# Block-sparse attention and a three-way feed-forward on one core: early PSUM banks, first weight landings, register loads and planner times changed

## The chip, the cores and the metric

One core of a Trainium2 chip runs the whole program. Its engines are TensorE (PE, with its weight loads counted apart as PEld), VectorE (DVE), ScalarE (ACT), GpSimd (POOL) and the queue of SyncE (SP), which issues most transfers. The metric is the device time of one execution in microseconds, as the median of several runs.

## The reference

Attention over 4 batches of 8 heads with 768 positions of 64 values, in blocks of 32 positions. A block of queries sees its own block and its two neighbours, the first and the last block, and three sampled blocks; the first and the last block of queries see everything. The attention's rows (3072 x 512) then go through a feed-forward with three weight matrices, of whose products the elementwise maximum is taken, and an output matrix.

```python
mask = np.abs(blk_i - blk_j) <= window
mask = mask | (blk_i == 0) | (blk_j == 0) | (blk_i == n_blocks - 1) | (blk_j == n_blocks - 1)
...
scores = np.where(mask, scores, -1000000000.0)
...
return np.matmul(attn, v).astype(np.float32)
...
h = np.maximum(np.maximum(x @ w1, x @ w2), x @ w3)
return (h @ w_out).astype(np.float32)
```

## The kernel before, in words

Every operand of a matmul is held as two float16 parts, a high one and a low one (the rest), after a scaling by a power of two; a product is three passes (high-high, high-low, low-high, `PASSES`). So each fp32 input is first brought into such parts: K, Q and V, and the weights.

**Units.** A batch has 12 units of 64 query rows. Eleven are sparse: unit m takes blocks 1+2m and 2+2m. One, "G", takes the first and the last block against all keys. Their order is G, 10, 8, 9, then 0 to 3, then 4 to 7. A sparse unit gathers its key blocks on chip (`gather`, line 746: per unit six copies of sampled blocks at line 757, one for each of two query blocks and three samples, and two window copies at lines 763 and 765, into tile `kg`) and its value rows from a copy of V in DRAM (`vscr`) by indirect DMAs of the GpSimd queue (line 769, into `vg`). Two items of four heads each follow: scores on PE into a pair of PSUM banks (line 844), row maxima (DVE, line 823), the bias (ACT, line 825), exponentials (ACT, line 853), the high part (ACT, line 801), the low part (POOL or DVE, line 802 or its alternative), a transposing DMA (SP, line 806) into `pts`, and the product with the values (PE, line 868). The global unit does the same with all keys (`global_items`, lines 889 to 923); the first one is turned on PE in place of the DMA (line 794). `finish_unit` (line 933) divides, turns the 64 rows on PE into a PSUM bank (line 950), and writes both parts into `xg`. Every fourth unit completes 256 rows, and a feed-forward follows (`feed_forward`, line 961): 18 groups of 12 matmuls (line 977), and 6 groups for the output (line 1004). There are 12 of them.

**The start.** Constants; the sampled block numbers are loaded into tile `samp`, and from there into engine registers (`registers`, line 396; the load is line 393), which the copies of line 757 use as offsets. Each engine needs registers of its own. Batch 0's K, Q and V land in `stage` and `qn`; their scales come from sums of squares on PE (`gram`, line 422, matmuls at line 430; `total`, line 412, line 418) and a few tiny DVE operations (lines 405 to 410, 607, 706, 707). K and Q are turned on PE (line 602 in the first batch) and evicted by ACT (high part: lines 630 and 719) and DVE (low part: 633 and 722). V's parts are made by ACT (line 648) and DVE (line 652) and stored to `vscr` (line 656). `edges` (line 729) copies the first and last key block into both `kg` buffers (DVE, line 735) and the same of V into both `vg` (SP, line 741).

**Weights.** `prep_weights` takes eight groups of three 512 KB pieces: six groups of w1, w2 and w3, two of w_out. A piece lands by DMA (lines 472 and 475), is decoded (POOL or ACT, lines 479 and 482; DVE, line 486), summed (lines 430 and 418), and split into high (ACT, line 508) and low parts (DVE, line 520, or POOL, lines 518 and 519). `stage_of` says where piece t lands: pieces 0 and 1 in `xg` buffers 1 and 2, then in turn in the six `stage` tiles (also those of K and V) and one `xg`.

**PSUM.** Two score tiles `s_ps0` and `s_ps1` of two banks each, `av_ps`, two banks `f_ps` of the feed-forward, and `tp_ps`. In the planner the score tiles' banks are 0 to 3 and `tp_ps` is 4. A score item takes a pair, (0, 1) or (2, 3). A turn or sum takes a single: bank 4, and while its priority is below `early` = 4, also bank 3 or 2, the two halves of `s_ps1`.

**The order of the work.** Nothing is ordered by hand. Every operation is given to `Plan.add` (line 57) with its engine, an estimated duration `us`, the keys that it reads and writes, a priority `pri` (lower is earlier), for transfers a time `land` from issue to landing and a share `move` of DMA time, and with `alts` other engines that could do it. `Plan.order` (line 81) plays the list through: it gives each engine, whenever it is free, the ready operation of lowest priority; among alternatives it takes the one that ends first. What results is the fixed program order on each engine; on the chip each instruction still waits for its semaphores. `Plan.gaps` finds where PE stands idle in the plan, and `idle` puts dummy matmuls there (line 1079).

Of the kernel before, what the change touches and what calls it, by code (L numbers as in the profile page):

```python
# [32 lines left out]
TP, HOLD, WPRI, WSL = 0.45, 1.0, 1.5, 0.65  # L33
# [10 lines left out]
class Plan:  # L44
# [6 lines left out]
    SEM, DEPTH, START, COLD = 0.15, 2, 2.0, 3.0  # L51
    PACKET, FETCH, QUEUE = 256, 2.2, 0.8

    def __init__(self, early):
        self.ops, self.wrote, self.readers, self.early = [], {}, {}, early

    def add(self, eng, us, emit, r=(), w=(), pri=0.0, land=None, mode=None, move=0.0, take=None, pair=False, drop=None, free=(), port=0, fresh=None, alts=(), n=24, half=False):
# [20 lines left out]
        self.ops.append(Op(eng=eng, us=us, emit=emit, deps=deps, pri=pri, land=land, mode=mode, move=move, take=take, pair=pair, drop=drop, port=port, fresh=fresh, seen=seen, n=n, half=half,  # L78
                           alts=[(eng, us, emit, port), *alts] if alts else ()))

    def order(self, hold, switch):
# [6 lines left out]
        dma, lock, banks = 0.0, 0.0, [0.0] * 5  # L88
# [41 lines left out]
        while len(out) < n:  # L130
# [92 lines left out]
def tile_block_sparse_attention_maxout_ffn(ctx, tc, q, k, v, sampled, w1, w2, w3, w_out, out):  # L223
# [69 lines left out]
    FAR = 1e6  # L293
# [153 lines left out]
    w_first = [(xg[i].rearrange("p g t x -> p (g t x)").bitcast(F32), XK(i)) for i in range(1, 3)]  # L447
    w_first += [(vgf[i][:, 1024 * x : 1024 * x + 1024], VGK(i)) for x in range(2) for i in (1, 0)][:0]
# [53 lines left out]
    def split_w(g, parts, sc, keys, pri):  # L502
        m3, hi, lo, mk = parts
        for k in range(3):
# [11 lines left out]
            else:  # L516
                def low(sl=sl, s=s):
# [4 lines left out]
                    r=keys + [("w", g, k, 0)], w=mkk + [("w", g, k, 1)], pri=pri, port=1, alts=[("POOL", 3.2, low, 0)] if 1 else ())  # L522
# [42 lines left out]
    def load_v(x, b, pri, after):  # L565
        sts = []
        for a in range(3):
# [5 lines left out]
            ), r=after, w=SK(i), pri=pri, land=2.2, move=2.05)  # L573
# [68 lines left out]
    def prep_v(b, pri, after=()):  # L642
        sm = vsm[b % 3]
        sts = load_v(v, b, pri, after)
        kv_scale(sts, sm, "v", b, pri)
        for a in range(3):
# [4 lines left out]
            for e in range(2):  # L651
# [3 lines left out]
                    r=SK(sts[a]) + [("v", "s", b), ("vh", a)], w=[("vl", a, e)], pri=pri, port=1)  # L655
# [382 lines left out]
    F = 0  # L1038
# [77 lines left out]
```

## Time and profile before

| | |
|---|---|
| median of 3 runs | 665.83 us (665.64 to 666.9) |
| the profiled execution, its own time | 669.87 us |
| its span in the trace | 668.1 us |
| mean granted TensorE clock | 0.971 |
| PE busy | 607.5 us, 11033 matmuls (233 of them dummies, 33.5 us) |
| DVE, ACT, POOL busy | 401.9, 415.7, 323.0 us |
| moved by DMA | 105.09 MB |

Times in views are microseconds from the span's start. "L977" is line 977 of the kernel. A view of waits names for each instruction the event that released it; "issue" stands where the engine waited for nothing that the profile shows. A granted clock of 1.00 is full speed.

### The profile page before, as it was taken

What the parts mean: (1) busy time and instruction counts of PE and PEld (TensorE: products, weight loads), DVE (VectorE), ACT (ScalarE), POOL (GpSimd) and SP (SyncE); (2) the same over time, 40 slices, a digit from 0 to 9 for tenths busy, and PEclk for the clock granted to TensorE, in tenths of its full rate; (3) what the DMA queues carried; (4) which work ended last, traced back from release to release, by engine and by line L of the source; (5) the groups of instructions that cost most, each with busy time, mean ns of one, the idle gap of its engine ahead of it and who ended that gap; (6) DMA issues with size and microseconds to landing.
All of it is one profiled execution on the core that took longest, in us unless ns stands there. A gap on an engine that the chain in (4) does not pass through costs nothing.

```text
span 668.1 us, 26145 instructions
## 1 busy us (share of the span) xinstructions
PE 607.5 (91%) x11033; PEld 459.8 (69%) x11033; DVE 401.9 (60%) x963; ACT 415.7 (62%) x898; POOL 323.0 (48%) x414
## 2 busy tenths in 40 slices
PE   6697877989999899999999998999998899988997
PEld 5575556866776676866867756868866768657684
DVE  2386889997775564665766555656865547435221
ACT  0365767898678565685778655775776566635211
POOL 3114755845536473455366644554365565625110
PEclk9897779999999899999999998999999999999999
DMA  7679999999769999997579897863589874784100
GB/s 194 190 235 245 210 226 164 198 196 210 128 99 216 169 161 193 178 164 157 118 179 197 154 191 163 187 154 93 143 186 165 149 167 91 128 124 89 37 14 31
DMA packets 194567, 105.09 MB, mean 157 GB/s; under 512 B 154785, under 2 KB 181522, under 8 KB 194450
## 3 DMA queue, kind: packets, MB, share of 16 engines
q1 hardware_dynamic: 186002, 74.13, 61.0%
q0 software_dynamic: 8448, 29.29, 18.3%
q8 instruction: 86, 1.41, 0.9%
q14 instruction: 31, 0.25, 0.2%
HBM read 62.91 MB, written 12.70 MB: 113 GB/s over the span
## 4 chain that ended last, share of the span: by engine, by line
PE 68%; DMA 9%; issue 7%; DVE 6%; ACT 5%; ACTq 2%; POOL 1%; another core or an unknown queue 1%; SPq 0%; DVEq 0%; POOLq 0%
PE f_ps L977 37%; PE f_ps L1004 11%; PE av_ps L868 6%; DMA pts<-phl 6%; PE s_ps L844 5%; PE tp_ps L599 3%; DMA vg<-vscr,rows_of 2%; ACTq L393 2%; DMA vscr<-vhl 1%; ACT pr L853 1%; PE tp_ps L950 1%; PE s_ps L889 1%; ACT phl L801 1%; PE s_ps L602 1%; PE f_ps L1079 1%
## 5 line engine op out<-in xcount | busy, mean ns | idle before, releaser
L977 PE MATMUL f_ps<-xg,w_hl 128*128 128x256 f16 x2592 | 304.4, 274 | 7.4 <-issue 5.4
L977 PEld LDWEIGHTS <-w_hl 128*128 128x128 f16 x2592 | 249.2, 98 | 48.2 <-issue 17.1
L802 POOL TENSOR_TENSOR phl<-pr,phl 128x512 f16<-128x512 f32 (+1 forms) x112 | 128.8, 1154 | 112.7 <-ACT phl L801 52.4
L990 POOL TENSOR_TENSOR ht<-hf,ht 128x256 f16<-128x256 f32 x72 | 51.8, 719 | 124.8 <-ACT ht L989 123.9
L986 DVE SCALAR_TENSOR_TENSOR hf<-f_ps,hf 128x256 f32<-128x256 f32 x144 | 60.8, 422 | 79.3 <-PE f_ps L977 72.4
L769 POOL DMA_INDIRECT vg<-vscr,rows_of x88 | 84.2, 956 | 48.6 <-PE av_ps L868 27.8
L1004 PE MATMUL f_ps<-wo_hl,ht 128*128 128x512 f16 x432 | 99.4, 379 | 1.3 <-DVE hf L986 1.3
L853 ACT ACTIVATE pr<-s_ps,nm,qsm 128x256 f32<-128x256 f32 x176 | 92.7, 561 | 6.8 <-ACT nm L825 0.4
L823 DVE TENSOR_REDUCE nm<-s_ps 128x2 f32<-128x512 f32 x88 | 59.6, 686 | 32.7 <-PE s_ps L844 27.5
L1004 PEld LDWEIGHTS <-ht 128*128 128x128 f16 x432 | 40.9, 98 | 46.2 <-issue 3.2
L801 ACT CAST phl<-pr 128x512 f16<-128x512 f32 (+1 forms) x112 | 66.7, 596 | 5.4 <-DMA pts<-phl 3.2
L868 PE MATMUL av_ps<-vg,pts 128*32 128x65 f16 (+1 forms) x4224 | 51.9, 197 | 12.5 <-issue 8.2
L868 PEld LDWEIGHTS <-pts 128*32 128x32 f16 x4224 | 41.6, 96 | 30.4 <-issue 24.6
L989 ACT CAST ht<-hf 128x256 f16<-128x256 f32 x72 | 28.9, 401 | 53.6 <-DVE hf L986 53.5
L825 ACT ACTIVATE nm<-nm,ln_top,qsm 128x2 f32<-128x2 f32 x88 | 34.0, 386 | 43.4 <-DVE nm L823 43.4
L844 PE MATMUL s_ps<-kg,qt 64*32 64x256 f16 x2112 | 49.7, 286 | 7.0 <-issue 4.3
L982 ACT ACTIVATE hf<-f_ps 128x256 f32<-128x256 f32 x72 | 27.5, 382 | 33.2 <-PE f_ps L977 30.6
L773 DVE COPY vg<-vg 32x2080 f16<-32x2080 f16 x44 | 38.2, 868 | 11.2 <-DMA vg<-vscr,rows_of 10.1
L757 POOL COPY kg<-kt 128x256 f16 x88 | 38.6, 460 | 12.9 <-DVE kt L633 12.0
L757 ACT COPY kg<-kt 128x256 f16 x104 | 38.0, 402 | 3.2 <-issue 1.5
L844 PEld LDWEIGHTS <-qt 64*32 64x32 f16 x2112 | 25.2, 93 | 20.8 <-issue 14.9
L1079 PE MATMUL f_ps<-ident 128*128 128x256 f16 x233 | 33.5, 299 | 0.0
(164 smaller groups left out, 690.2 us busy)
## 6 DMA issues: line engine op xcount, KB each, us to landing
stage<-in_moe_w_dram SPq DMA_DIRECT2D x14, 511.0 KB
vscr<-vhl SPq DMA_DIRECT2D x12, 520.0 KB
stage<-in_v_dram SPq DMA_DIRECT2D x12, 512.0 KB
out_dram<-ob SPq DMA_DIRECT2D x20, 256.0 KB
stage<-in_k_dram SPq DMA_DIRECT2D x18, 256.0 KB
qn<-in_q_dram SPq DMA_DIRECT2D x17, 256.0 KB
stage<-in_moe_w_out_dram SPq DMA_DIRECT2D x5, 511.8 KB
vg<-vscr SPq DMA_DIRECT2D x16, 130.0 KB
```

The lines of the kernel that those rows point to most:

```text
L757: (A.copy if by == 2 else eng.tensor_copy)(out=dst, in_=src)
L769: plan.add("POOL", 1.02, lambda c=c: L.indirect_dma_start(out=vgj[: (6 - 2 * c) * HB, c].rearrange("p e h x -> p (e h x)"), out_offset=Non ...
L801: plan.add("ACT", 0.05 + 0.565 * n / 512, lambda: A.copy(out=hl[:, :n], in_=prt[:, :n]), r=PRK(it), w=[hk], pri=pri, alts=[("DVE", 0.6 * n ...
L802: plan.add("POOL", 1.2 * n / 512, lambda: L.tensor_tensor(out=hl[:, n : 2 * n], in0=prt[:, :n], in1=hl[:, :n], op=ALU.subtract), r=PRK(it) ...
L823: plan.add("DVE", 0.7, lambda: V.tensor_reduce(out=n[:, 0:2], in_=both()[:, :, :256], axis=AX.X, op=ALU.max), w=[ks, (ks, 0), (ks, 1)], pr ...
L844: T.matmul(out=s_ps[r * BS : (r + 1) * BS, hd * 512 : hd * 512 + 256], lhsT=q_t[hp, tq, 2 * i + u, q0 + c * BS : q0 + (c + 1) * BS], rhs=k ...
L853: plan.add("ACT", 0.56, lambda hd=hd: A.activation(out=prt[:, hd * 256 : hd * 256 + 256], in_=s_of(job)[:, hd * 512 : hd * 512 + 256], fun ...
L868: T.matmul(out=av_ps[r * BS : (r + 1) * BS, 2 * i + hd, :w], lhsT=pv[:, tp, hd, e, r * BS : (r + 1) * BS], rhs=vgj[:, c, e, h, (D + 2) * t ...
L977: T.matmul(out=pf, lhsT=w_hl[f][:, j, g, wp], rhs=x[:, g, xp, :], start=g == 0 and n == 0, stop=g == G - 1 and n == 2)
L986: plan.add("DVE", 0.42, lambda h=h, pf=pf: V.scalar_tensor_tensor(out=h, in0=pf, scalar=2.0 ** -14, in1=h, op0=ALU.mult, op1=ALU.max), r=[ ...
L990: plan.add("POOL", 0.7, lambda h=h, hi=hi, lo=lo: L.tensor_tensor(out=lo, in0=h, in1=hi, op=ALU.subtract), r=[hk, ("ht", f)], w=[("htl", f ...
L1004: T.matmul(out=f2_ps, lhsT=hts[:, f, hp, t * P : (t + 1) * P], rhs=wo_hl[f // 3][:, f % 3, wp], start=f == 0 and n == 0, stop=f == NF - 1 ...
```

## The change

Nothing of what is computed changes. The edits:

- Early singles: `early` goes from 4 to 3, and the banks offered become 4 (`tp_ps`), 5 (`f_ps1`, for operations numbered below `plan.first`), 2 and 0 (the first halves of `s_ps1` and `s_ps0`). `plan.first` is set to 1 after `prep_v(0)`. Operations that free a bank before that are readers of a key "first", on which the first matmuls into `f_ps1` depend.
- Weight pieces 2 and 3 land in `wo_hl[1]` and `wo_hl[0]`, tiles that later hold the output weights.
- Registers: sample 0 goes to DVE (was ACT for the first units), sample 1 stays with POOL, sample 2 with ACT; each loads 8 at first, and POOL and ACT six more in twos. The copies of sample 0 for units 1 to 8 go from ACT to DVE.
- Weights' low parts lose the alternative POOL; batch 0's V low parts get one, in two POOL operations.
- Planner times: transposing DMAs are planned to land 1.5 us later and gathers 2.0 us later (`slack`), the bias operation takes 0.38 in place of 0.22, the modelled depth of SP's queue is 1.5 in place of 2.
- Priorities: weights from 1.5 to 1, unit ends from 5 to 7 ahead, edges from 0.3 to 1 behind, K of the next batch two units earlier, V's loads of batches 2 and 3 released two units later and with the same resulting priority.

```diff
-TP, HOLD, WPRI, WSL = 0.45, 1.0, 1.5, 0.65
+TP, HOLD, WPRI, WSL = 0.45, 1.0, 1, 0.65
...
-    SEM, DEPTH, START, COLD = 0.15, 2, 2.0, 3.0
+    SEM, DEPTH, START, COLD = 0.15, 1.5, 2.0, 3.0
...
             deps.add(drop["op"])
+            if not self.first:
+                self.readers.setdefault("first", []).append(i)
...
-            return [(banks[j], -j, 1) for j in ((4, 3, 2) if ops[i].pri < self.early else (4,))]
+            return [(banks[j], -j, 1) for j in (4, 5, 2, 0) if (ops[i].pri < self.early if j < 4 else j == 4 or i < self.first)]
...
-                done = max(dma, done) + op.land
+                done = max(dma, done) + op.land + op.slack
...
-    plan = Plan(4)
+    plan = Plan(3)
...
-        return tp_one if j == 4 else s_pss[1][:, 512 * (j - 2) : 512 * (j - 1)]
+        return tp_one if j == 4 else f_ps[1] if j == 5 else s_pss[j // 2][:, :512]
...
+    w_late = [wo_hl[1], wo_hl[0], *w_hl[:0:-1]]
+    w_first += [(x.rearrange("p j g t x -> p (j g t x)" if len(x.shape) == 5 else "p f t x -> p (f t x)").bitcast(F32)[:, :1024],
+                 [("w", g, k, t) for k in range(2) for t in range(2)])
+                for g, x in zip((NF + 1, NF, *range(NF - 1, 0, -1)), w_late)][:2]
...
-                    r=keys + [("w", g, k, 0)], w=mkk + [("w", g, k, 1)], pri=pri, port=1, alts=[("POOL", 3.2, low, 0)] if 1 else ())
+                    r=keys + [("w", g, k, 0)], w=mkk + [("w", g, k, 1)], pri=pri, port=1, alts=[("POOL", 2.85, low, 0)] if 0 else ())
...
+        def low_v(x, hi, lo):
+            L.tensor_scalar(out=x, in0=x, scalar1=sm[:, 8:9], scalar2=None, op0=ALU.mult)
+            L.tensor_tensor(out=lo, in0=x, in1=hi, op=ALU.subtract)
...
-                    r=SK(sts[a]) + [("v", "s", b), ("vh", a)], w=[("vl", a, e)], pri=pri, port=1)
+                    r=SK(sts[a]) + [("v", "s", b), ("vh", a)], w=[("vl", a, e)], pri=pri, port=1, alts=[("POOL", 2.85, lambda src=src, a=a, e=e: low_v(src[:, e], vhl[:, a, e, :, :D], vhl[:, a, e, :, D + 2 :]), 0)] if 1 and not b else ())
...
-                by = (2,1,2)[t] if pri < 8 else t
+                by = (0,1,2)[t] if pri < 8 else t
...
-            ), r=VSCR(b) + ["rows_of"] + pace, w=[("vg", j % 2, c)], pri=pri, land=2.5, move=1.6 - 0.5 * c)
+            ), r=VSCR(b) + ["rows_of"] + pace, w=[("vg", j % 2, c)], pri=pri, land=2.5, move=1.6 - 0.5 * c, slack=2.0)
...
-            r=[hk, lk], w=[tk, ("ptl", it % NPT)], pri=pri - 2, land=2.0, move=1.75 * n / 512)
+            r=[hk, lk], w=[tk, ("ptl", it % NPT)], pri=pri - 2, land=2.0, move=1.75 * n / 512, slack=1.5)
...
-        plan.add("ACT", 0.22, lambda: A.activation(
+        plan.add("ACT", 0.38, lambda: A.activation(
...
-        pri -= 5
+        pri -= 7
...
-                         w=[("f1", fb)] + [("pace", F, x) for x in range(4) if (f, j) == ((0, 0), (1, 1), (3, 0), (4, 1))[x]], pri=pri, mode="f", fresh=fb)
+                         w=[("f1", fb)] + [("pace", F, x) for x in range(4) if (f, j) == ((0, 0), (1, 1), (3, 0), (4, 1))[x]],
+                         free=["first"] if F == f == 0 and j == 1 else (), pri=pri, mode="f", fresh=fb)
...
-        by = (2,1,2)[t] if 8 > 0 else t
-        registers(t, by, many if by else many[:8], -9 + t / 10)
+        by = (0,1,2)[t] if 8 > 0 else t
+        first = 8 if by else 8
+        registers(t, by, many[:first], -9 + t / 10)
+        for x in range(first, len(many) if by else first, 2):
+            registers(t, by, many[x : x + 2], 0.5)
...
     prep_v(0, PV)
+    plan.first = 1
...
-            edges(b, U + 0.3)
+            edges(b, U + 1)
...
-        if x == max(gx, 4 if U < 12 else 3) and b + 1 < B:
-            prep_v(b + 1, U + 7, [("unit", U)])
+        if x == max(gx, 4 if U < 12 else 5) and b + 1 < B:
+            prep_v(b + 1, U + 5, [("unit", U)])
...
-            prep_k(b + 1, U + 2, [("unit", U)])
-            turn_k(b + 1, U + 2 + 1)
+            prep_k(b + 1, U + 0, [("unit", U)])
+            turn_k(b + 1, U + 0 + 1)
```

More of the change, by code (lines that the diff above doesn't have):

```diff
@@ L44, with add @@
 class Plan:
-    SEM, DEPTH, START, COLD = 0.15, 2, 2.0, 3.0
+    SEM, DEPTH, START, COLD = 0.15, 1.5, 2.0, 3.0
     PACKET, FETCH, QUEUE = 256, 2.2, 0.8
     def __init__(self, early):
-        self.ops, self.wrote, self.readers, self.early = [], {}, {}, early
-    def add(self, eng, us, emit, r=(), w=(), pri=0.0, land=None, mode=None, move=0.0, take=None, pair=False, drop=None, free=(), port=0, fresh=None, alts=(), n=24, half=False):
+        self.ops, self.wrote, self.readers, self.early, self.first = [], {}, {}, early, 0
+    def add(self, eng, us, emit, r=(), w=(), pri=0.0, land=None, mode=None, move=0.0, take=None, pair=False, drop=None, free=(), port=0, fresh=None, alts=(), n=24, half=False, slack=0.0):
         i = len(self.ops)
@@ L77, in add @@
             take.update(op=i, left=0, end=0.0)
-        self.ops.append(Op(eng=eng, us=us, emit=emit, deps=deps, pri=pri, land=land, mode=mode, move=move, take=take, pair=pair, drop=drop, port=port, fresh=fresh, seen=seen, n=n, half=half,
+        self.ops.append(Op(eng=eng, us=us, emit=emit, deps=deps, pri=pri, land=land, mode=mode, move=move, take=take, pair=pair, drop=drop, port=port, fresh=fresh, seen=seen, n=n, half=half, slack=slack,
                            alts=[(eng, us, emit, port), *alts] if alts else ()))
@@ L87, in order @@
         ready, cands, free, last = [0.0] * n, {}, {}, "f"
-        dma, lock, banks = 0.0, 0.0, [0.0] * 5
+        dma, lock, banks = 0.0, 0.0, [0.0] * 6
         pos, since, back, kept = 0, -9.0, 0.0, None
@@ L284, in tile_block_sparse_attention_maxout_ffn @@
     tp_one = ps.tile([P, 512], F32, name="tp_ps")
-    plan = Plan(4)
+    FAR = 1e6
+    plan = Plan(3)
     def bank(job):
         j = job["banks"][0]
-        return tp_one if j == 4 else s_pss[1][:, 512 * (j - 2) : 512 * (j - 1)]
+        return tp_one if j == 4 else f_ps[1] if j == 5 else s_pss[j // 2][:, :512]
     V, A, T, Y, L = nc.vector, nc.scalar, nc.tensor, nc.sync, nc.gpsimd
-    FAR = 1e6
     SK = lambda i: [("stage", i), ("stage2", i)]
@@ L572, in load_v @@
                 in_=x[b, :, a * 256 : (a + 1) * 256, :].rearrange("h (p e) d -> p h (e d)", e=2),
-            ), r=after, w=SK(i), pri=pri, land=2.2, move=2.05)
+            ), r=after, w=SK(i), pri=pri if b else min(pri, 9), land=2.2, move=2.05)
         return sts
@@ L903, in global_items @@
                  r=[("nm", its[1] % 4)], w=[ks], pri=pri)
-        plan.add("ACT", 0.22, lambda: A.activation(
+        plan.add("ACT", 0.38, lambda: A.activation(
             out=n[:, 2:4], in_=n[:, 0:2], func=AF.Identity, bias=ln_top, scale=sm[:, 5:6]),
```

## The prediction

> **What bounds the kernel now.** I read the time by stage first. The three rows give TensorE's (PE's) busy time in the start, the middle and the tail (columns: stretch, length, then busy us and count for PE, weight loads, VectorE (DVE), ScalarE (ACT), GpSimd (POOL), granted clock, DMA share, GB/s). The fence behind them is the same view for line 1079 alone, dummy matmuls that fill gaps (PE and weight loads, clock, DMA).
>
> ```profile
> span 668.1 us, 26145 instructions
> 0.00:110.00 110.00, 80.71 (x1274) 61.45 (x1275) 72.05 (x166) 60.04 (x115) 46.37 (x81) 0.86 0.88 211
> 110.00:640.00 530.00, 502.56 (x9576) 380.34 (x9575) 326.01 (x789) 350.75 (x772) 273.27 (x328) 0.99 0.83 154
> 640.00:668.10 28.10, 24.24 (x187) 18.01 (x185) 3.82 (x9) 4.93 (x11) 3.34 (x5) 0.97 0.05 19
> ```
>
> ```profile
> 0.00:110.00 110.00, 31.02 (x215) 22.65 (x215) 0.86 0.88 211
> ```
>
> In the first 110 us PE does 80.71 - 31.02 = 49.7 us of useful work and loses 60.3. In the next 530 it idles 27.4 us, in the tail 3.9. Two thirds of all that PE loses lies in the start; afterwards PE itself sets the pace. So the start is read next, by the chain of waits (start, length, what).
>
> ```profile
> 2.01 0.21 ACTq L393
> ...
> 18.05 0.15 ACTq L393
> 18.35 0.84 ACT qt L719
> 19.21 0.80 DVE qt L722
> 20.04 0.69 ACT kt L630
> 20.77 1.60 PE s_ps L602 x16
> 22.47 0.76 DVE kt L633
> ...
> 36.38 0.61 DVE kg L735 x2
> ...
> 38.29 0.56 DVE kg L735 x2
> ...
> 41.43 2.08 DVE vhl L652 x3
> 43.56 8.53 DMA vscr<-vhl
> 53.00 12.41 DMA vg<-vscr,rows_of
> ```
>
> ACT's queue loads registers (L393) up to 18.35. Then the turned Q and K are evicted one engine at a time until 36.38, four small edge copies (L735) lie ahead of V's low halves (L652), V goes to DRAM, and only then can the first gather begin. The timeline (start, length, engine, line, operation; idle time and releaser in brackets) shows what the two long pieces wait for, and where the start ends.
>
> ```profile
> 14.12 1.04 PE L602 MATMUL s_ps<-ident,stage 128*64 128x128 f32 x16
> 14.22 0.15 DVE L707 TENSOR_SCALAR qsm<-qsm 128x1 f32<-128x1 f32 x1
> 18.35 0.83 ACT L719 ACTIVATE qt<-s_ps,qsm 128x512 f16<-128x512 f32 x1 [16.13 <-issue]
> 22.47 0.75 DVE L633 SCALAR_TENSOR_TENSOR kt<-s_ps,ksm,kt 128x512 f16<-128x512 f32 x1 [1.84 <-PE s_ps L602]
> 109.60 2.67 PE L977 MATMUL f_ps<-xg,w_hl 128*128 128x256 f16 x23 [1.93 <-DVE xg L955]
> ```
>
> The scales stand at 14.37, and K's second turn is in PSUM at 15.16; ACT comes 4 us later. At 22.47 VectorE waits 1.84 us for a PE write into the other half of tile s_ps, though what it reads was written at 14.12. The whole chain from 18.35 to 36.38 goes on like this: PE, ACT, DVE, never two at once on that tile. The Trainium skill (PSUM — Partial Sum Buffer, "PSUM bank collisions raise a hardware error") lets only two engines on one bank clash, and a half of 512 fp32 is its "2 KiB" bank; by it nothing in the chip asks for these waits, and with own tiles they would go whole. The first feed-forward (L977) starts at 109.60, released by the fourth unit's output (L955).
>
> **The change part by part.** The busy time of two stretches of the start, same columns as above:
>
> ```profile
> 18.35:36.40 18.05, 11.72 (x130) 10.02 (x134) 8.47 (x18) 7.73 (x11) 1.36 (x3) 0.81 0.57 177
> 80.00:109.60 29.60, 21.84 (x524) 15.36 (x523) 24.62 (x52) 21.49 (x44) 18.43 (x21) 0.78 1.05 212
> ```
>
> Registers. ACT loads 14 + 14 blocks before its first eviction: 16.13 us, 0.576 each. Afterwards 8, so it is free at about 2.0 + 4.6 = 6.8, and the eviction waits for the scales at 14.37: -4.0. DVE takes eight (4.6 us from about 2.0), where the chain of waits does not touch it before 19.21; without that cover they cost up to 4.6. POOL has 8 ahead instead of 14. Six more on ACT and on POOL come in twos at priority 0.5, between other work; DVE loads its own when a copy first needs them.
>
> Own tiles. Early single banks are now tp_ps and the first halves of both score tiles. In 18.35 to 36.40 the busiest engine is PE with 11.72 us, so at most 6.3 of the 18.05 us can go and, if another engine's order keeps the turns apart, nothing. I take -5.0, near the upper end, because the waits stand in the rows. The price is that an early single now blocks a score pair on either tile, where before s_ps0 was always free: between 0 and one eviction pair (1.5 us) on the path; 0 taken, as no scores are ready before K is turned. Bank 5, half of f_ps[1], is offered only to an operation numbered below plan.first = 1; operation 0 is the constants, which need no bank. So it is never used, and the new dependence of the first f_ps[1] matmul on early drops is met long before 109.60: 0.
>
> Edges, priority 0.3 to 1. Their two pairs leave the chain ahead of L652: 0.61 + 0.56 = -1.2. What they release are the first sparse unit's scores and values; their four DMAs go behind more weight loads on SP. The cover is that unit's gather, which lands at 53.00 + 12.41 = 65.41; without it the 1.2 us would come back there.
>
> V's low halves may go to POOL, weights' may not. The rows (median in the middle of three ns figures; or count, us, mean ns):
>
> ```profile
> L652 DVE SCALAR_TENSOR_TENSOR vhl<-stage,vsm,vhl x24: 739/744/1403, 39.4 to 484.7; 128x512 f16<-128x512 f32 x24
> L518 POOL TENSOR_SCALAR kt<-kt,w_s 128x512 f32<-128x512 f32 x1 | 1.6, 1579 | 3.0 <-ACT w_hl L508 3.0
> L519 POOL TENSOR_TENSOR w_hl<-kt,w_hl 128x512 f16<-128x512 f32 x1 | 1.2, 1164 | 0.1
> L757 DVE COPY kg<-kt 128x256 f16 x72 | 22.7, 338 | 9.4 <-issue 9.2
> L757 DVE COPY kg<-kt x72: 210/227/1174, 139.1 to 604.1; 128x256 f16 x72
> ```
>
> Beside six lows of 0.744 on DVE, POOL can do one in 2.74: -0.7; a POOL low that ends last would cost up to 2.0 instead. So far V's store moves by 4.0 + 5.0 + 1.2 + 0.7 = 10.9 us, to about 32.7.
>
> What eats into that is DVE. Sixteen copies (units 1 to 8) move from ACT to it; I count ten before the first feed-forward, at 0.338 = 3.4; one weight low comes back from POOL, 0.74; two of its registers are loaded late, 2 x 0.576 = 1.15. That is 5.3 us, on an engine busy 24.62 of 29.60 us, so 83% of it, +4.4, lies on the path. Bounds: nothing, if ACT's relief is what counts, and 13.6, where each copy takes the longest 1.174. The feed-forward then starts 6.5 us earlier, near 103.
>
> Weights. Two more landing places (2 x 511 KB) and half a unit earlier priority: their loads fill DMA time that is idle now (share 0.57 in the row above), their splits go ahead of unit work. One group is six DVE passes of the size of L652's 0.744, so between -4.4 and +4.4 for the fourth unit; 0 taken, since the first feed-forward needs earlier both weights and rows.
>
> The middle: waits for transposes and gathers are planned 1.5 and 2.0 us longer, unit ends and K's preparation come earlier, V's of two batches two units later. PE's waits after 120 us (total, times, longest):
>
> ```profile
> PE av_ps L868 <- issue: 8.2, 9, 3.2
> PE f_ps L977 <- issue: 5.4, 7, 2.5
> PE av_ps L868 <- DMA pts<-phl: 3.9, 4, 2.5
> PE av_ps L923 <- DMA pts<-phl: 2.0, 1, 2.0
> ```
>
> Only 5.9 us are DMA waits, which the slack addresses; 13.6 are "issue", which no edit touches. I take a third of the 5.9, -2.0, with -5.9 and +4 (an order with two more of the longest stalls, 3.2 + 2.5, less the 2.0) as bounds. The longer bias estimate and the shallower queue model change only the planner's choices: 0, inside the same bounds.
>
> Sum: -6.5 - 2.0 = -8.5 us. The profiled execution took 669.87 us (span 668.1 and 1.8 around it), 0.6% over the median of 665.83. In its measure the result is 661.4; scaled, 665.83 x (1 - 8.5/669.87) = 657.4.
>
> **The rivals.** *The gain stops at the weights for the output.*
>
> ```profile
> 149.68 2.59 PE f_ps L1004 x12
> L520 DVE SCALAR_TENSOR_TENSOR wo_hl<-kt,w_t,wo_hl x6: 742/743/1643, 147.6 to 150.9; 128x512 f16<-128x512 f32 x6
> stage<-in_moe_w_dram SPq DMA_DIRECT2D x14, 511.0 KB
> ```
>
> The first output matmul (L1004) already runs as the last weights are split. If they come no earlier, the first feed-forward's 6.5 us are given back before 150 unless other units fill them; with nothing gained in the middle either, 665.8. Against it: weights rank 0.5 earlier.
>
> *DMA paces the start.* With a share of 1.05 from 80 to 110 us, only transfers moved into the idle DMA time before count: two loads of 511 KB at 177/0.57 = 310 GB/s, 3.3 us: 662.5. Against it: what releases L977 at 109.60 is VectorE, not a DMA.
>
> *Singles and pairs collide.* The tiles' gain goes, as turns and scores block each other, and -4.0 - 1.2 - 0.7 + 4.4 - 2.0 = -3.5 stays: 662.3. It is the case too if the missing bank 5 was what the order needed.
>
> *Slower: DVE becomes the bound at units 1 to 5.* Each of the ten copies runs into a POOL operation and takes 1.174: 11.7 + 0.74 + 1.15 = 13.6, whole on the path, against 10.9 gained, and one weight group pushed ahead of the fourth unit adds 4.4; with the middle unchanged that is +7.1, or 673. It decides from a mean copy of about 0.9 us without the weight group, 0.46 with it; the row has 0.338. This is what the Trainium skill's rule (SBUF — State Buffer, "Who interferes with whom") would make of it: a copy in a two-port mode and a GpSimd operation hold one port in turn, and the later one "fully blocks". The trace agrees that some copies do (1174 against a median of 227 ns), not that most do.
>
> **How the numbers follow.** Forecast 0.58; output weights 0.10; DMA 0.08; collision 0.06; slower 0.18 (with any other order that stalls more). The forecast's own ends are -10.9 - 5.9 = -16.8 (649) and -6.5 + 4 = -2.5 (663.3). The whole range, 649 to 667.5, leaves out most of the slower rival and little below. A difference of 0.2% (1.3 us) is what a measurement of this kernel can tell from none. Faster by more: 0.58 + 0.08 + 0.06 = 0.72; within: 0.10; slower: 0.18.
>
> **What would show it.** ACT's first eviction near 14.4 in place of 18.35; no alternation on s_ps up to 36.38, K turned by 28; V's store issued near 33, the first gather near 42, L977 near 103; line 1079 under 30 us. PE's DMA waits after the start are down, "issue" is not. I am wrong if L977 starts no earlier than 108, if DVE's copies average over 0.5 us, or if idle PE after 120 us grows by more than the start gives.

## The result and the profile after

| | before | after |
|---|---|---|
| median of four runs each | 665.74 us | 646.87 us (644.22 to 650.74) |
| the profiled execution, its own time | 669.87 us | 647.59 us |
| its span | 668.1 us | 645.8 us |
| mean granted TensorE clock | 0.971 | 0.976 |
| dummy matmuls | 233, 33.5 us | 193, 29.7 us |

The ratio is 0.9724, 95% interval 0.9668 to 0.9779: 18.9 us faster, where 8.5 were forecast and 16.8 was the far end of the range. Ratios here leave disturbed executions out; the profiles read for the registers alone, for the kernel without slack and for the changed kernel with shifted blocks are of disturbed ones.

The start first. The timeline of the changed kernel, from the first eviction to the first feed-forward (start, length, engine, line, operation, in brackets the idle time before it and who ended it):

```profile
14.78 0.69 ACT L636 ACTIVATE kt<-s_ps,ksm 128x512 f16<-128x512 f32 x1 [12.56 <-PE s_ps L608]
15.43 1.04 PE L608 MATMUL tp_ps<-ident,qn 128*64 128x128 f32 x16
15.49 1.62 DVE L639 SCALAR_TENSOR_TENSOR kt<-s_ps,ksm,kt 128x512 f16<-128x512 f32 x2 [0.92 <-ACT kt L636]
16.52 0.84 ACT L730 ACTIVATE qt<-tp_ps,qsm 128x512 f16<-128x512 f32 x1 [0.19 <-PE tp_ps L608]
...
24.66 0.75 DVE L639 SCALAR_TENSOR_TENSOR kt<-s_ps,ksm,kt 128x512 f16<-128x512 f32 x1 [0.41 <-ACT kt L636]
...
33.21 1.07 SPq L667 DMA_DIRECT2D vscr<-vhl  x1
...
42.71 1.17 POOL L780 DMA_INDIRECT vg<-vscr,rows_of  x1 [7.66 <-DMA vscr<-vhl]
...
94.26 0.85 PE L879 MATMUL av_ps<-vg,pts 128*32 128x65 f16 x48 [6.79 <-DMA pts<-phl]
...
103.05 1.47 PE L988 MATMUL f_ps<-xg,w_hl 128*128 128x256 f16 x12
```

ACT waits for PE now and no longer for its registers (12.56 us where it was 16.13); PE turns Q into one tile while ACT and DVE read the other; K is turned by 25.4; V's last store is issued at 33.21, the first gather at 42.71, the first feed-forward starts at 103.05. The view of groups by form gives the copies that went to DVE in one row (count, us, mean ns):

```profile
L768 DVE COPY kg<-kt 128x256 f16 x88 | 27.8, 338 | 2.9 <-issue 2.6
```

The mean is 338 ns, as it was. So the start went as the prediction has it, and it gives 109.60 - 103.05 = 6.55 us. The span fell by 22.3. Of that, 3.4 us are not the change's: the profiled execution of before took 4.1 us more than the median (669.87 against 665.74), that of the changed kernel 0.7. Where the other 15.75 are, the busy time of both kernels after that point tells (before, then after; columns as in the prediction):

```profile
107.39:668.10 560.71, 527.47 (x9766) 398.81 (x9763) 332.44 (x801) 357.16 (x786) 277.89 (x335) 0.99 0.79 147
```

```profile
103.05:645.80 542.75, 526.02 (x9774) 398.93 (x9773) 330.73 (x801) 354.18 (x777) 275.41 (x334) 0.99 0.77 149
```

(107.39 is one early matmul of L977; the row of 109.60 is the second.) PE works as long as it did, 526.0 against 527.5 us. Its idle time falls from 33.2 to 16.7 us. The view of PE's waits after the start shows which waits went. First two lines of before that the prediction's cut of this view leaves out, then the changed kernel:

```profile
PE s_ps L844 <- issue: 2.7, 7, 0.8
...
PE tp_ps L418 <- issue: 0.3, 1, 0.3
```

```profile
PE f_ps L988 <- issue: 3.1, 3, 2.3
PE av_ps L879 <- issue: 2.1, 6, 0.5
PE tp_ps L961 <- DVE kt L639: 1.6, 2, 0.8
PE s_ps L855 <- issue: 1.2, 3, 0.7
```

In the changed kernel no wait for a transposing DMA is left (5.9 us before), and "issue" is 3.1 + 2.1 + 1.2 = 6.4 us; before it was 8.2 + 5.4 + 2.7 + 0.3 = 16.6. The two falls, 5.9 and 10.2, are 16.1 of the 16.5 us of idle time. The first was forecast at 2.0 with 5.9 as its bound, the second at nothing. The experiments therefore ask three things: do the steps of the start hold one by one, is the middle's gain the settings' doing or that of the one order they led to, and what is "issue"?

### The profile page after: what moved, and what is told of

It reads as the page before. It is cut to its first block, busy times and chain, and to the rows that moved or that the text cites. A ratio compares the mean times of both kernels' runs of the same rounds, so it can differ in the third digit from the quotient of the medians.

```text
span 645.8 us, 26024 instructions
## 1 busy us (share of the span) xinstructions
PE 597.3 (92%) x10993; PEld 452.7 (70%) x10993; DVE 402.0 (62%) x979; ACT 414.2 (64%) x886; POOL 317.7 (49%) x410
## 4 chain that ended last, share of the span: by engine, by line
PE 71%; issue 2%; ACT 2%; DVE 2%; ACTq 0%
PE f_ps L988 41%; PE f_ps L1016 13%; PE av_ps L879 5%; PE s_ps L855 5%; PE tp_ps L605 3%; PE tp_ps L961 2%; PE av_ps L934 1%; PE s_ps L900 1%; PE tp_ps L420 1%; ACT ob L1022 1%; ACT pr L921 1%; ACT pr L864 0%; DVE vhl L663 0%; DVE kt L639 0%; DVE nm L834 0%
## 5 line engine op out<-in xcount | busy, mean ns | idle before, releaser
L1002 POOL TENSOR_TENSOR ht<-hf,ht 128x256 f16<-128x256 f32 x72 | 51.8, 720 | 104.9 <-ACT ht L1001 97.5
L879 PE MATMUL av_ps<-vg,pts 128*32 128x65 f16 (+1 forms) x4224 | 50.4, 196 | 9.6 <-DMA pts<-phl 7.2
L855 PE MATMUL s_ps<-kg,qt 64*32 64x256 f16 x2112 | 46.2, 276 | 5.2 <-issue 1.9
L768 POOL COPY kg<-kt 128x256 f16 x88 | 37.3, 445 | 6.6 <-PE s_ps L855 3.3
L768 ACT COPY kg<-kt 128x256 f16 x88 | 32.5, 404 | 5.9 <-PE s_ps L855 4.6
L965 ACT CAST xg<-tp_ps 128x256 f16<-128x256 f32 x41 | 15.2, 370 | 26.8 <-PE tp_ps L961 21.9
```

What stands on the lines that cost most here:

```text
L768: (A.copy if by == 2 else eng.tensor_copy)(out=dst, in_=src)
L855: T.matmul(out=s_ps[r * BS : (r + 1) * BS, hd * 512 : hd * 512 + 256], lhsT=q_t[hp, tq, 2 * i + u, q0 + c * BS : q0 + (c + 1) * BS], rhs=k ...
L879: T.matmul(out=av_ps[r * BS : (r + 1) * BS, 2 * i + hd, :w], lhsT=pv[:, tp, hd, e, r * BS : (r + 1) * BS], rhs=vgj[:, c, e, h, (D + 2) * t ...
L1002: plan.add("POOL", 0.7, lambda h=h, hi=hi, lo=lo: L.tensor_tensor(out=lo, in0=h, in1=hi, op=ALU.subtract), r=[hk, ("ht", f)], w=[("htl", f ...
```

## The experiments

### The steps of the start, in the old order

Both edits change only what is emitted; the order that the planner chose for the kernel before stays.

```diff
 def registers(t, by, js, pri):
     def load():
-            for i in js:
+            for i in js[:8]:
```

The remaining registers are loaded when a copy first needs them. 

> The kernel before with its order of work unchanged; only the register blocks at the start load 8 in place of 14 each (the other six at their first use). ACT then has 16 loads in place of 28 ahead of its first eviction: it starts near 2.0 + 16 x 0.576 + 0.5 = 11.7, that is, as soon as the scales stand (14.4 in place of 18.35). Forecast's step: the chain's end at V's store and the first feed-forward move by up to 4.0 us, and the time too if nothing takes it back (661.8). Rival, the start's gain is given back later in a fixed order: the first eviction moves, the time stays within 1.5 us.

Measured: 1.0046 (0.9989 to 1.0103). No gain. The timeline of ACT in this kernel:

```profile
15.67 0.83 ACT L719 ACTIVATE qt<-s_ps,qsm 128x512 f16<-128x512 f32 x1 [13.45 <-PE s_ps L602]
...
17.36 0.69 ACT L630 ACTIVATE kt<-s_ps,ksm 128x512 f16<-128x512 f32 x1 [0.33 <-DVE qt L722]
21.97 0.76 ACT L482 CAST ob<-xg 128x512 f16<-128x512 bf16 x1 [3.92 <-DMA xg<-in_moe_w_dram]
22.60 0.82 ACT L719 ACTIVATE qt<-s_ps,qsm 128x512 f16<-128x512 f32 x1
```

The first eviction is 2.7 us earlier (18.35 before). The fourth operation in ACT's queue is the decoding of a weight piece, and its transfer lands when it did; ACT now waits 3.92 us for it, with K's evictions queued behind. K's last eviction starts at 35.46, before at 35.63. In this fixed order the earlier registers gain nothing; what they are worth in a new order no run shows by itself.

The own tiles alone: bank 3 of the preparation of batch 0 is taken from the other score tile.

```diff
 def bank(job):
     j = job["banks"][0]
+        if j == 3 and job["op"] < plan.start:
+            return s_pss[0][:, :512]
...
+    plan.start = len(plan.ops)
```

> The kernel before with its order of work unchanged; only bank 3 of batch 0's preparation lies in the other score tile, so that the three early singles are in three tiles. Forecast's step: the waits from engine to engine on one tile go, the last eviction of K ends 5 us earlier (31.4 in place of 36.4), the time falls by up to 5 us. If the order of each engine, and not the tile, keeps the turns apart: the end stays at 36 and the time within 1.5 us.

Measured: 0.9883 (0.9828 to 0.9937). K's last eviction in this kernel:

```profile
29.90 0.75 DVE L635 SCALAR_TENSOR_TENSOR kt<-s_ps,ksm,kt 128x512 f16<-128x512 f32 x1 [0.86 <-PE s_ps L432]
```

That is 5.7 us earlier than 35.63, where the prediction took 5.0 and had 6.3 as the most, and V's first store follows (34.89, before 40.91). What went are the waits on the shared tile: between 14 and 37 us VectorE waited 8.7 us for PE's writes into s_ps, and with own tiles 0.9. How much of the time this is worth is less certain than the ratio's interval says: by the plain medians of all executions it is 664.38 against 668.34, 0.994. Both edits in one kernel:

> Both of the two edits above, order still unchanged: by the forecast's steps K's last eviction ends near 27 us and the first feed-forward starts up to 9 us earlier (near 100), the time is near 657; if the order of the later work, made for other landing times, gives the gain back, the first feed-forward starts earlier and the time stays above 662.

Measured: 0.9934 (0.9884 to 0.9984), K's last eviction at 30.50, not near the 27 expected. The register edit adds nothing to the tiles that these runs could tell.

### One part of the change taken back, the order drawn anew

The planned landings without their `slack`:

```diff
-land=2.5, move=1.6 - 0.5 * c, slack=2.0)
+land=2.5, move=1.6 - 0.5 * c)
...
-land=2.0, move=1.75 * n / 512, slack=1.5)
+land=2.0, move=1.75 * n / 512)
```

> The changed kernel with the planner's added landing times taken out again (slack 0 for the gathers and the transposing DMAs). Theory A, the later planned landings made the middle's gain of 15.7 us: the first feed-forward still starts near 103 us, idle PE after it goes from 16.7 back to about 30 us, and the time is near 660 us. Theory B, the priorities made it: within 3 us of 646.9. Theory C, the changed kernel's order is one lucky draw and any other order loses: 655 to 662 us here and in the other three runs alike.

The priorities of before:

```diff
-TP, HOLD, WPRI, WSL = 0.45, 1.0, 1, 0.65
+TP, HOLD, WPRI, WSL = 0.45, 1.0, 1.5, 0.65
...
-        pri -= 7
+        pri -= 5
...
-            edges(b, U + 1)
+            edges(b, U + 0.3)
...
-            prep_v(b + 1, U + 5, [("unit", U)])
+            prep_v(b + 1, U + 7, [("unit", U)])
...
-            prep_k(b + 1, U + 0, [("unit", U)])
+            prep_k(b + 1, U + 2, [("unit", U)])
```

> The changed kernel with the old priorities (weights 1.5, unit ends 5 ahead, edges 0.3, K and V of the next batch as before). Theory A: within 3 us of 646.9. Theory B: idle PE after the start back to about 30 us, near 660 us. Theory C: 655 to 662 us.

The early singles of before:

```diff
-            return [(banks[j], -j, 1) for j in (4, 5, 2, 0) if (ops[i].pri < self.early if j < 4 else j == 4 or i < self.first)]
+            return [(banks[j], -j, 1) for j in ((4, 3, 2) if ops[i].pri < self.early else (4,))]
...
-    plan = Plan(3)
+    plan = Plan(4)
...
-        return tp_one if j == 4 else f_ps[1] if j == 5 else s_pss[j // 2][:, :512]
+        return tp_one if j == 4 else s_pss[1][:, 512 * (j - 2) : 512 * (j - 1)]
...
```

> The changed kernel with the old early singles (tp_ps and both halves of s_ps1, early 4, no dependence of the first f_ps1 matmul). The forecast's step of 5 us for own tiles: the waits from engine to engine on s_ps are back while K and Q are evicted, the first feed-forward starts near 108 us, and the time is near 652 us. If the tiles were worth nothing, the start stays near 103 and the time within 2 us of 646.9. Theory C: 655 to 662 us.

And, as a measure for these, the changed kernel with nothing taken back: only the planner's estimate of a semaphore is another, which no edit of the change touches, so that it draws another order.

```diff
-    SEM, DEPTH, START, COLD = 0.15, 1.5, 2.0, 3.0
+    SEM, DEPTH, START, COLD = 0.16, 1.5, 2.0, 3.0
```

> The changed kernel with one planner constant moved by a hair (the assumed time of a semaphore, 0.16 in place of 0.15), which means nothing on the chip but lets the planner choose another order. Theories A and B: within 4 us of 646.9, first feed-forward near 103 us. Theory C, a lucky order: 655 to 662 us, with idle PE after the start near 30 us.

Measured, each against the kernel before on the same chip: without slack 0.9848 (0.978 to 0.9917), old priorities 0.9939 (0.9896 to 0.9983), old banks 0.9953 (0.9912 to 0.9995), and the other order alone 0.9867 (0.9791 to 0.9943). Every one of them loses 1.2 to 2.3% against 0.972, the one in which nothing was taken back as well. That is theory C, that any other order loses: by these ratios the four take 656 to 663 us. So a part's worth can't be read from taking it back once: a new order alone costs 1.5%. (With the old banks the first feed-forward starts at 104.9, where the forecast's step for own tiles would have it near 108.) How much an order scatters had to be measured.

### Other orders, with the new settings and with the old

Three more orders under the new settings (0.17, 0.145 and 0.155 for a semaphore), three under the old ones (0.16, 0.14 and 0.155), and the changed kernel once more.

> The changed kernel with the planner's semaphore time at 0.17 in place of 0.15: a second draw of another order. The first one (0.16) lost half of the gain. If the edits set the level and the draw only scatters round it: 647 to 656 us. If the changed kernel's order is an outlier of its own settings, as low as no other draw: 653 us or more again.

> The kernel before with the planner's semaphore time at 0.16 in place of 0.15, so another order from the same settings. Draws of the changed kernel's settings gave ratios of 0.972 (itself), 0.987 and 1.003. Theory C, the order's draw is worth as much as the edits: this draw, too, is over 0.7% from the kernel before, either way. Theory D, only the changed kernel's settings scatter, because the added landing times and priorities make its plan tight: within 0.7%.

> The same with 0.14: a third draw of the old settings. Theory C: the three old draws spread by 1% to 2%, with a mean above that of the new draws. Theory D: all within 0.7%.

> The changed kernel with 0.145: a fourth draw of the new settings. Theory C: anything from 0.97 to 1.005. If the edits set the level and 0.17 was the outlier: 0.972 to 0.99.

> The changed kernel, whose order is chosen with 0.155 us for a semaphore in place of 0.150: a fifth order under the new settings. Theory that settings and draw count about alike: 0.975 to 1.0, mean of the new draws stays near 0.986. Theory that the settings make the whole gain (A): 0.967 to 0.98. Theory that only the draw counts: as often above 0.996 as below.

> The kernel before with 0.155 us for a semaphore: a fourth order under the old settings. Settings and draw alike: 0.985 to 1.01. If only the draw counts, orders such as 0.975 are found here too.

> The changed kernel itself once more. If the order it has is good by itself (theory C, its own draw) the ratio repeats at 0.967 to 0.978, with issue waits of TensorE after the first feed-forward of 4 to 9 us and no wait for a transposing DMA. If 0.972 was the chip of that day, the ratio goes to 0.985 or more.

Measured (columns: ratio with its interval; then from the trace, in us: start of the first feed-forward, and of the gaps above 0.25 between PE's matmuls after it those called issue, of these those at a block's end, which a later part explains, and those put down to a transposing DMA):

```
settings, semaphore   ratio [95%]               first FF  issue  at blocks  transposes
new, 0.15             0.9724 [0.9668, 0.9779]   103.0     5.6    3.4        0
new, 0.15 again       0.9703 [0.9652, 0.9755]    98.0     9.1    6.5        0
new, 0.145            0.9839 [0.9790, 0.9888]   100.3     4.1    4.1        0
new, 0.155            0.9827 [0.9776, 0.9878]    98.5    11.0    7.5        0.4
new, 0.16             0.9867 [0.9791, 0.9943]    89.5    10.2    7.1        0
new, 0.17             1.0031 [0.9969, 1.0094]    90.7    16.1   12.5        0
old, 0.15             1                         107.4    16.0    9.7        5.9
old, 0.14             0.9944 [0.9902, 0.9985]   106.4     6.3    6.3        0
old, 0.155            1.0082 [1.0045, 1.0120]   106.4    11.3    7.3        0.7
old, 0.16             0.9945 [0.9913, 0.9977]   102.2    10.7   10.7        2.3
```

The changed kernel's ratio repeats on another chip. Its two rows are two executions of the same program, and they differ by 5 us in the start and by 3.5 us in issue: a row tells of one execution, and smaller differences between rows tell nothing. Its five orders (the first two rows are one, 0.971) average (0.971 + 0.984 + 0.983 + 0.987 + 1.003) / 5 = 0.986, the four of the old settings 0.999. By these means the settings are worth 0.986 / 0.999, some 1.3% or 9 us, with a standard error of about 0.6%, so that with so few orders no effect at all is not quite ruled out. Nor is it known whether 0.15 was a draw like the others; without it the means are 0.989 and 0.999. The order that the changed kernel has is 0.971 / 0.986, another 1.5% or 10 us. Two more things stand in the table. Start and end are not tied: the two orders with the earliest feed-forward, 89.5 and 90.7, are the slowest under the new settings. And the waits for transposes are gone with the later planned landings, but two of the old orders nearly lack them too. That their going need not bring a gain shows the kernel before with `slack=1.5` on the transposes and nothing else, its order drawn anew:

> The kernel before with one edit alone: the transposing DMAs are planned to land 1.5 us later. Theory A, it takes away PE's waits for transposes: the 5.9 us of such waits after the start of the feed-forward fall below 1 us in its trace, whatever the total does. By itself that would be worth up to 5.9 us, 660; the draw of the order may add or take 7 us.

Measured: 1.011 (1.0047 to 1.0173). The waits for transposes are gone, and PE loses as much elsewhere:

```profile
PE av_ps L879 <- issue: 12.5, 7, 4.0
PE s_ps L855 <- issue: 5.1, 4, 2.3
PE av_ps L879 <- DMA vg<-vscr,rows_of: 3.8, 2, 2.6
```

"Issue" alone is 17.6 us in these lines. This is one draw, so it does not show what the slack is worth on the average. What varies most from order to order is this wait, 4 to 18 us.

### What "issue" is

The longest one of the kernel before, in the timeline of PE:

```profile
410.01 0.48 PE L868 MATMUL av_ps<-vg,pts 128*32 128x65 f16 x39
413.73 0.34 PE L868 MATMUL av_ps<-vg,pts 128*32 128x65 f16 x9 [3.24 <-issue]
```

PE stops for 3.24 us inside one item's 48 matmuls, between the 39th and the 40th, where nothing can be waited for. In the trace's records of the instruction queue (86 packets of 16 KB) one begins at 411.09. So instructions were being fetched. First theory: transfers hold the fetches up. From the 41st item on, this kernel moves only half the bytes of each transposing DMA: it leaves out the low half of the probabilities.

```diff
-            out=ptt[:, : 2 * n].rearrange("p (n x) -> p n x", x=P),
-            in_=hl[:, : 2 * n].rearrange("p (n x) -> p n x", x=P), transpose=True),
+            out=ptt[:, : (2 if it < 40 else 1) * n].rearrange("p (n x) -> p n x", x=P),
+            in_=hl[:, : (2 if it < 40 else 1) * n].rearrange("p (n x) -> p n x", x=P), transpose=True),
```

> The kernel before, same order on the four compute engines; from the 41st item on only the high half of the probabilities is moved by the transposing DMAs and the low half is left as it stood. Theory that TensorE's issue waits are instruction fetches held up by transfers: DMA share of the middle falls from 0.79 to about 0.65, issue after the start from 16.6 to under 9 us, time by about 8 us (0.988), the DMA waits of 5.9 us gone as well (0.98 with both). Rival, that issue comes from the order of instructions alone: issue stays at 14 to 19 us and the ratio at 0.99 to 1.0, by the DMA waits only.

Measured: 0.998 (0.9944 to 1.0016). The busy time of 110 to 640, its waits after 115, and the same place:

```profile
110.00:640.00 530.00, 509.23 (x9652) 387.40 (x9650) 327.87 (x792) 353.36 (x778) 276.25 (x330) 0.99 0.66 135
```

```profile
PE av_ps L868 <- issue: 7.7, 9, 3.5
PE f_ps L977 <- issue: 4.6, 5, 2.8
PE av_ps L868 <- DMA pts<-phl: 2.2, 1, 2.2
PE s_ps L844 <- issue: 2.0, 6, 0.5
```

```profile
404.92 0.48 PE L868 MATMUL av_ps<-vg,pts 128*32 128x65 f16 x39
408.89 0.26 PE L868 MATMUL av_ps<-vg,pts 128*32 128x65 f16 x9 [3.49 <-issue]
```

The DMA share fell from 0.83 to 0.66, the waits for transposes from 5.9 to 2.2, and issue stayed at 14.3, where the theory had under 9; the long one is at the same matmul. So halving the transposes' bytes does not take these waits away; that other transfers add to them is not ruled out.

That it is the same matmul suggested counting. If all of PE's instructions in the trace (weight loads, matmuls, and also the semaphore waits and drains of its queue) are numbered from 0, the matmuls behind the six issue waits of at least 0.79 us between 100 us and the end (1.62, 0.98, 0.79, 3.24, 2.51, 1.75) have the numbers 2498, 9154, 10178, 13762, 20674 and 21186. Divided by 256 each leaves 194. In each of the six PE goes on 2.4 to 2.9 us after a fetch began, however long the wait. In all 20 profiles of the study the rests 193 and 194 carry 40 to 100% of the issue time after the first feed-forward (60% in both kernels compared); what makes the others, of up to 1.2 us each, is not shown. The Trainium skill (Runtime: NRT & Kernel Launch, "Instruction fetch mechanics") says that an engine's instructions are refilled in blocks of 16 KB, 256 of them, and that crossing a block's end is "mostly hidden". The trace agrees with the first (86 packets for 22117 instructions, one in 257), and with "mostly": of the 77 ends after 100 us seven show more than 0.25 us. But those seven cost 11.3 us.

The kernel before says as much. Its planner has a term for these waits, and the changed kernel has the same one:

```python
    PACKET, FETCH, QUEUE = 256, 2.2, 0.8
...
                late = max(0.0, since + self.FETCH + self.QUEUE * back - at)
...
                        if fetched(t, ops[i].us, ops[i].n, pos, since, back)[0] > 0.1:
                            now = ffn
```

At every 256th PE instruction by its own count it plans a wait if too little time has passed since the last one, and it puts feed-forward work ahead of attention work that would run into a wait of over 0.1 us. So by the kernel's own model these waits depend on the order, and every edit of the planner's inputs can move them. How near the planned places come to the chip's was not measured; the count takes in an estimate of the dummy matmuls.

If so, the place in the stream makes the wait, not the work. The test moves the blocks and leaves the order as it is: 64 small matmuls with their weight loads, half a block, ahead of PE's first.

```diff
     with tc.manual_schedule():
+        shift = True
         for _, i in sorted(plan.times):
+            if shift and plan.ops[i].eng == "PE":
+                x, shift = ident.bitcast(F16), False
+                for _ in range(64):
+                    T.matmul(out=f_ps[0][:32, :8], lhsT=x[:, :32], rhs=x[:, :8], start=True, stop=True)
             if i in gaps:
```

> The kernel before, with 64 matmuls of 8 columns and their weight loads ahead of the first matmul of TensorE (which waits for its load until 6.2 us), the rest of each engine's order unchanged. Theory that a place in the instruction stream makes the issue waits: the three largest, of 3.2, 2.5 and 1.8 us, leave their matmuls, others of the same sort come up elsewhere, and all again at a rest of 193 or 194 of the stream counted with the new instructions; their sum is some other number between 4 and 18 us, so that the time moves by up to 7 us down or up (0.99 to 1.01). Rival, that the work makes them: they stay at the same matmuls with about the same lengths, now at a rest of 65 or 66, and the ratio is 0.998 to 1.002.

Measured: 0.995 (0.9912 to 0.9988), 3.3 us faster. The start, the old place of the long wait, and the one long wait that there is now:

```profile
2.44 1.87 PE L1087 MATMUL f_ps<-ident 128*32 128x8 f16 x64 [2.44 <-DVE ident L307]
5.92 1.01 PE L430 MATMUL tp_ps<-qn 128*128 128x128 bf16 x8 [1.62 <-DMA qn<-in_q_dram]
...
268.40 0.39 PE L977 MATMUL f_ps<-xg,w_hl 128*128 128x256 f16 x2
271.49 1.77 PE L977 MATMUL f_ps<-xg,w_hl 128*128 128x256 f16 x8 [2.70 <-issue]
...
409.70 0.56 PE L868 MATMUL av_ps<-vg,pts 128*32 128x65 f16 x48
```

The 64 matmuls run while PE waits for its first load. The 48 matmuls of the old place are in one piece again (409.70), all six long waits have left their matmuls, and the two new ones at blocks' ends, 2.70 us at number 8642 and 0.82 us at number 12738, leave 194 again. That is not the scatter of executions: in the four other kernels with PE's old order (the three of the start and the one with half transposes) the waits at 13762 and 20674 come back, with 3.5 to 4.2 and 2.2 to 2.8 us. One wait of 1.20 us stays where 0.55 was before, at a matmul that stands at no block's end (rest 98, now 226). At the blocks' ends 3.8 us remain of 9.7, of issue 9.3 of 16.0. Of these 6.7 us about half is seen in the time: PE's idle time after the first feed-forward falls by 4.4 us, since its other waits grow by 2.3. In this profile the first feed-forward also starts 4.9 us earlier (102.51 for 107.39), of which the wait of 1.62 that is gone explains a part, so the time does not price the middle alone. That the place makes the long waits is shown; why the fetch begins late at one end in ten is not.

The same 128 instructions in the changed kernel ask whether its few waits are luck of this kind.

> The changed kernel with the same 128 instructions ahead of its first matmul, the rest of the order unchanged. If its small sum of such waits (3.4 and 6.5 us in two profiles, where most orders have 8 to 14) was the luck of where the blocks fall, it goes to 8 to 14 us and the ratio from 0.971 to 0.976 to 0.985. If the order itself keeps TensorE fed, ratio 0.967 to 0.975 and issue 4 to 7 us as before.

Measured: 0.9771 (0.9719 to 0.9824); issue 6.6 us, 3.3 of it at the blocks' ends. The waits speak for the second expectation: they stay small with the blocks elsewhere. The ratio lies in the range of the first, with an interval that reaches into the second and overlaps that of the changed kernel, and decides nothing. Waits for transposes, which the changed kernel had none of, are back with 3.7 us in this profile.

## Why the prediction was right and wrong

- *Registers, -4.0; own tiles, -5.0; edges, -1.2; V's low half, -0.7.* Right in the changed kernel: first eviction 3.6 us earlier, K turned at 25.4 where "by 28" was forecast, the last store at 33.21 for "near 33". In the fixed order the tiles' 5.7 us were shown on their own; the waits that went are those of two engines on one tile, as the prediction read from 22.47. The registers alone gained nothing: the time that they freed went behind the cast of a weight. What they add in the new order, and the small parts, were not tried alone.
- *DVE's extra 5.3 us, of which 4.4 on the path.* The copies took 338 ns as costed, and the first feed-forward came at 103.05 for "near 103". That the sum is right doesn't show that this term is: the path there holds a wait of 6.79 us for a transpose at 94.26, which the prediction did not have. And a second execution of the same program starts it at 98.02, so that the hit to 0.1 us is luck.
- *The slower rival, DVE as the bound.* It needed copies of 0.46 us or more; they stayed at 0.338. Of the 88 copies 26 took over 0.35 us, and each of these began while POOL was at work, as the rival had it; they were too few.
- *Output weights, DMA, collision.* The first two would have held the gain at 665.8 and 662.5. The last low half of the output weights starts at 142.9 (150.9 before), and the time went below both. No run tried the third by itself.
- *The middle, -2.0.* This step failed. It held that 13.6 us are "issue", "which no edit touches", and so put that term at nothing. In its own two lines these 13.6 fell to 5.2. With the two lines that it left out, 16.6 fell by 10.2 to 6.4 us (10.4 us are left in the second execution), and the waits for transposes fell by 5.9, not by a third of that. The view calls issue what it cannot put down to anything, and the prediction took that for something fixed, though it granted a new order up to 4 us more of it and the kernel's own planner has a term for it. The runs show what the larger part of it is, a stream cut every 256 instructions, and that it moves with the order of the work: from 4 to 18 us over the orders measured, with nearly the same instructions to run. An edit that redraws the order touches all of it.
- *The size of a redraw.* As an effect of its settings the change is worth about 9 us by the mean of the orders, with 4 us of standard error. That is close to the 8.5 forecast, but it may be by chance: the parts in the middle were not separated. The rest goes with the one order drawn: with 0.16 in place of 0.15 for a semaphore, and nothing else, half of the gain is gone. The prediction gave a new order a bound of +4 us to one side; the measured scatter is about 1.1% (7 us) under the new settings and 0.7% (4 us) under the old, to both. With that in it, the range would have reached below 647. The 0.2% that it took for what a measurement can tell was too fine as well; the intervals here reach 0.3 to 0.8% to either side.
- *What stays open.* Which setting makes the average better, why the changed kernel's order has so few of these waits under two positions of the blocks, and what the issue waits are that stand at no block's end (6.3 of 16.0 us before, 2.2 of 5.6 after).

## What to carry to other kernels

Where a planner sets the order, every edit of its inputs is also a new draw: measure the scatter, by changing a harmless constant, before crediting a part of one per cent to an edit, and keep the best draw as a gain of its own. When TensorE stops inside a run of equal matmuls and the profile names no releaser, number all instructions of its queue: if the stops share a rest by 256, and a record of the instruction queue begins 2 to 3 us before PE goes on, take them for instruction fetches. A few empty matmuls in a dead stretch at the front move them; here that gained 0.5% in one order and nothing that could be told in the other. An early release is worth nothing on an engine whose queue holds something that comes no earlier.

## What the runs showed of the hardware

- TensorE's stops at the end of a block of 256 instructions: 95 of over 0.6 us after the first 100 us of the 20 profiles, the longest of 4.9 us (old priorities). In 88 of them PE goes on 2.3 to 3.0 us after the last fetch before it began, in the other seven 3.2 to 5.5. Together such stops take 3 to 18 us a run, and 8.3 in place of 9.7 us with the DMA share at 0.66 in place of 0.83.
- 64 matmuls of 8 columns with weight loads of 32 took 1.87 us at the start of the program, 29 ns a pair.
- Copies on VectorE beside GpSimd: in the changed kernel 88 copies of 128x256 float16 have a median of 224 ns; the 26 of over 350 ns (up to 1456) all began while a GpSimd instruction ran, in the kernel before 20 of 72.
- Two engines on different banks of one tile wait for each other in this program, for 5.7 us of the start. The Trainium skill's rule on PSUM (PSUM — Partial Sum Buffer, "PSUM bank collisions raise a hardware error") asks for such a wait only on one bank. The run with own tiles agrees: the two halves then lie in different tiles, VectorE's waits on them fall from 8.7 to 0.9 us, and K's last eviction starts 5.7 us earlier.
